# Attention and expert layer on one core: operand addresses, accumulator banks, and where work at the two seams of the kernel stands

## The chip, the core and the metric

The kernel runs on one core of one Trainium2 chip. The core has a matrix engine (TensorE, "PE" in the profile, with its weight loads as "PEld"), a vector engine (VectorE, "DVE"), a scalar engine (ScalarE, "ACT"), GpSimd ("POOL") and a sync engine that issues most of the transfers ("SP"). The metric is the device time of one execution in microseconds (us), lower is better. Matrix products write to PSUM, eight banks of 512 fp32 numbers in each of 128 partitions; all other tiles lie in SBUF.

## The reference

```python
def _attn_ref(u, v, z):                       # 8 x 2496 x 256, z: 8 x 2496 x 64
    scores = (1.0 / S) * np.matmul(z, z.transpose(0, 2, 1))
    attn = np.maximum(scores, 0.0) ** 2
    return u * np.matmul(attn, v)

def _moe_ref(x, modality_id, w_gate, modality_bias, w1, w2):   # 19968 tokens, 8 experts
    logits = x @ w_gate + modality_bias[modality_id]
    e_idx = np.argmax(logits, axis=1)
    probs = softmax(logits)                   # with 1e-9 added to the sum
    gate_w = probs[np.arange(N), e_idx]
    for e in range(E):
        mask = e_idx == e
        h = np.maximum(x[mask] @ w1[e], 0.0)  # 256 x 1024
        out[mask] = gate_w[mask, None] * (h @ w2[e])
```

The attention's output, as 19968 rows of 256, is the input of the expert layer. Each token goes to one expert.

## The kernel before

**Precision.** Every fp32 operand of a product is split into a high part (rounded to fp32r) and a low part (the rest), and a product is the sum of three: high x high, high x low, low x high. So everything that feeds TensorE needs a cast (high, on ACT or DVE) and a subtraction (low, on DVE).

**Phase 1, attention.** A batch's 2496 rows are five chunks of 512 queries (the last one 448). A step `g` is one batch, one chunk, and two blocks of 128 keys; there are ten steps to a chunk, 400 in all. A step has these pieces:

- `scores(g)`: six matmuls (three pairs, one of each pair on either half of the rows) into one PSUM tile `s` of two banks, then a relu on ACT into `r` (L275).
- `square(g)` on ACT (L281), `high(g)` (`ah`, ACT or DVE, L288), `low(g)` (`al`, DVE, L297).
- `weigh(g)`: 24 products (L313) of `ah`, `al` with the value parts `vh`, `vl`, into four accumulators of one bank each: two halves of the model dimension (`dh`) times two halves of the rows (`r`). The first step of a chunk goes through all terms of `dh` = 0 first and then those of `dh` = 1; the others are sorted by operand.

At a chunk's end `evacuate_low` copies the two accumulators with `r` = 1 to SBUF (ACT, L355), `evacuate_high` adds the two with `r` = 0 (DVE, L359), `make_rows` turns the result by 16 matmuls (L389) into two PSUM tiles `po`, and `take_rows` multiplies by `u` (DVE, L399). Then `logits` computes the gate's logits on DVE, two products with an accumulated sum to a call (L411), 16 calls to a chunk. When a batch's logits are there, routing finds every token's slot among its expert's rows, and indirect transfers on POOL scatter the rows to a buffer `xs` in HBM (L524).

**PSUM.** `ps_s` holds `s` (two banks), `ps_a` six banks under one tag. `bank_tile` draws from `ps_a` for the accumulators, the `po` tiles, the small products of routing (`pc`), and the target of the products of zeros at the start (`warm`, L863). A tile waits for the last reader of the bank that it gets.

**Order.** The order on PE, ACT, DVE and POOL is the program's order (a manual schedule). Steps look ahead: later steps' scores are issued before a step's products, and at steps 1, 14 and 16 (`DEEPER`) the distance grows by one, so that one more `scores` is issued inside `weigh`, ahead of its last terms. Pieces beside the steps (evacuation, logits, splits of the next batch, routing) stand in a list `waiting` with a step by which they are due; `beside` places them by an estimated clock for ACT and DVE. What is left when the steps end is issued at once.

**Phase 2, experts.** 39 tiles of up to 512 tokens go through `run_tile`. The first four (t = -4 to -1) belong to the expert with most tokens so far, and start before the last tokens are routed. Slot `f` of a tile issues `up` (six matmuls, L983, relu into `hh` on ACT, L987, rest into `hl` on DVE, L988) for one eighth of the hidden width, then `down` of slot f - 2 (matmuls L996 and L997). `up` takes its PSUM tile from four banks. There are three sets of weight tiles; set 0 serves the tiles before t = 0 and every third after it. Weights are split in four parts each (`part_weights_high` on ACT, `part_weights_low` on DVE, L813): parts 0 and 1 are w1, 2 and 3 are w2. The first set is split in the last steps of phase 1. The list `between` holds work that is issued beside the first four tiles, by slot: the last chunk's rows (`make_last_rows`, L371, `take_last_rows`), its logits, two calls to a slot from slot 2 on, the routing of the last batch, and the planning of the remaining tiles.

**SBUF.** Pools stand one behind the other: `const`, `small`, `turned` (the `zm` tiles), `rows`, then `bulk` with `r`, `vh`, `vl`, `ah`, `al`. In phase 2 `mp` (`hh`, `hl` and others) and behind it `wp` (weight sets 1 and 2) take the place of `bulk`. Weight set 0 lies at the other end. A tile takes a multiple of 32 bytes of a partition.

The lines at the start of phase 1 that the change touches:

```python
        warm = [bank_tile([P, T], "warm") for _ in halves]
        for n in range(11):
            for x, h in zip(warm, halves):
                nc.tensor.matmul(out=x, lhsT=zeros[h, 0:P], rhs=zeros[h, :], start=True, stop=True)
```

Of the kernel before, what the change touches and what calls it, by code (L numbers as in the profile page):

```python
# [9 lines left out]
F32 = mybir.dt.float32  # L10
# [3 lines left out]
ALU = mybir.AluOpType  # L14
# [12 lines left out]
def tile_attention_moe(ctx: ExitStack, tc: tile.TileContext, u, v, zt, mid, wg, mb, w1, w2, out):  # L27
# [53 lines left out]
    turned = ctx.enter_context(tc.tile_pool(name="turned", bufs=1))  # L81
    rows = ctx.enter_context(tc.tile_pool(name="rows", bufs=1))
    bulk = ph1.enter_context(tc.tile_pool(name="bulk", bufs=1))
    raw = feed.enter_context(tc.tile_pool(name="raw", bufs=1, side="right"))
    ps_s = ph1.enter_context(tc.tile_pool(name="ps_s", bufs=1, space=PSUM))
    ps_a = ph1.enter_context(tc.tile_pool(name="ps_a", bufs=6, space=PSUM))
    bank = {"pool": ps_a, "tag": "acc"}

    def bank_tile(shape, name):
        return bank["pool"].tile(shape, F32, tag=bank["tag"], name=name)  # L90
# [172 lines left out]

    def scores(g):
        b, c, i = steps[g]
        w = width[c]
        s = ps_s.tile([P, 2, T], F32, tag="s", name="s")
        mv = Z[b, c]
        for n, (kl, ql) in enumerate(((0, 1), (1, 0), (0, 0)) if g else ((0, 0), (0, 1), (1, 0))):
            for t in range(2):  # L270
                k = 2 * i + t
                lhs = Z[b, k // J][halves[t], kl, (k % J) * P:(k % J + 1) * P]
                nc.tensor.matmul(out=s[:, t, :w], lhsT=lhs, rhs=mv[halves[t], ql, :w], start=n == 0, stop=n == 2)  # L273
        r = bulk.tile([P, 2, T], F32, tag="a", bufs=3, name="r")
        nc.scalar.activation(out=r[:, :, :w], in_=s[:, :, :w], func=AF.Relu, scale=INV)  # L275
        st_s[g] = r

    def square(g):
        w = width[steps[g][1]]
        a = st_s.pop(g)  # L280
        nc.scalar.square(out=a[:, :, :w], in_=a[:, :, :w])  # L281
        st_a[g] = a

    def high(g):
# [20 lines left out]
    def weigh(g, inside=()):  # L305
# [3 lines left out]
        if i == 0:  # L309
            acc[b, c] = list(zip(*([bank_tile([P, T], "acc") for _ in range(2)] for _ in range(KD))))  # L310

# [11 lines left out]
        terms = [(dh, x, y) for dh in range(KD) for x, y in ((ah, 0), (ah, 1), (al, 0))]  # L323
        if i:
            terms.sort(key=lambda t: (t[1] is al, t[2]))
        for m, (dh, x, y) in enumerate(terms):
            if m == len(terms) - KD:
                for n in inside:
                    scores(n)
            for k in (2 * i, 2 * i + 1)[:1 if last else 2]:  # L330
                for r in range(2):
                    product(r, dh, k, x, y)
        if last:
# [213 lines left out]
    def choose():  # L547

        cnt = t8("c_cnt")
        nc.vector.tensor_tensor(out=cnt, in0=base[one], in1=base0[one], op=ALU.subtract)  # L550
        most = small.tile([1, 1], F32, name="c_most")
        nc.vector.tensor_reduce(out=most, in_=cnt, axis=AX.X, op=ALU.max)
        val = t8("c_val")
        nc.vector.scalar_tensor_tensor(out=val, in0=cnt, scalar=most, in1=em8[one], op0=ALU.is_equal, op1=ALU.mult)
        who = small.tile([1, 1], F32, name="c_who")
        nc.vector.tensor_reduce(out=who, in_=val, axis=AX.X, op=ALU.min)
        nc.vector.tensor_scalar(
            out=skip, in0=em8[one], scalar1=who, scalar2=float(EARLY * T), op0=ALU.is_equal, op1=ALU.mult
        )
        at = small.tile([1, 2], F32, name="c_at")  # L560
        nc.vector.tensor_scalar(out=at[:, 0:1], in0=who, scalar1=float(E), scalar2=None, op0=ALU.add)
        nc.vector.tensor_scalar(out=at[:, 1:2], in0=at[:, 0:1], scalar1=float(CAP), scalar2=None, op0=ALU.mult)
        nc.vector.tensor_copy(out=first, in_=at)
# [287 lines left out]
    for q in range(KD + 2):  # L851
        queue(G - 8 + q, G - 4 + q, act(1.05, part_weights_high, -1, q), dve(1.25, part_weights_low, -1, q))
    queue(G - 6, G - 4, dve(1.2, turn_blocks, -EARLY), act(1.05, part_high, -EARLY), dve(1.25, part_low, -EARLY))
# [5 lines left out]
    with tc.manual_schedule(engines={ET.PE, ET.Activation, ET.DVE, ET.Pool}):  # L859
        warm = [bank_tile([P, T], "warm") for _ in halves]  # L860
        for n in range(11):
            for x, h in zip(warm, halves):
                nc.tensor.matmul(out=x, lhsT=zeros[h, 0:P], rhs=zeros[h, :], start=True, stop=True)  # L863
# [4 lines left out]
        prep_v_low(0, 0)  # L868
        square(0)
        by[0] = "D"  # L870
        high(0)
        low(0)
        scores(1)
        load_z(0, 3)
# [81 lines left out]
        for h in reversed(range(KD)):  # L956
            evacuate_high(B - 1, NCH - 1, h)
        waiting += [(end, g, p) for g in sorted(due) for end, p in due[g]]
        while waiting:
            waiting = [(0, 0, p) for _, _, p in waiting]  # L960
            beside(G, True)
# [140 lines left out]
    def put(slot, *pieces):  # L1102
        n, f = slots[slot]
        between[n][f] += pieces

    for n in range(LGN):
        put(2 + n // 2, lambda n=n: logits(B - 1, NCH - 1, n))
# [74 lines left out]
```

## Time and profile before

| | |
|---|---|
| median of three runs | 2264.76 us (2263.47 to 2266.08) |
| the profiled execution | 2264.21 us |
| its span in the trace | 2262.4 us |
| phase 1, to the last product | 0 to 1352 us |
| phase 2 | 1352 to 2262 us |
| PE, DVE, ACT, POOL busy | 99%, 80%, 70%, 16% of the span |
| granted clock of TensorE | 0.996 |

How to read the lines of the views. A line of the timeline is: start in us, length in us, engine, line of the kernel, operation, output <- inputs, number of instructions merged, and in brackets the idle time of the engine just before and what ended it. Matmuls overlap, so the distance between two starts says more than a length. A line of the waits is: engine, line, what was waited for, then total us, times, longest us. A line of the windows is: the stretch, its length, busy us and number of instructions of PE, PEld, DVE, ACT and POOL, then the granted clock of TensorE (1.00 is full), the share of the transfer engines, and GB/s. In the view of one source line, the last part lists who waited for that line's instructions: us in total and times.

### The profile page before, as it was taken

How to read it: one execution, taken by the hardware profiler on the slowest of the kernel's cores; microseconds unless marked ns; L12 is line 12 of the kernel's file. 1: busy time of each engine (PE TensorE's matmuls, PEld its weight loads, DVE VectorE, ACT ScalarE, POOL GpSimd, SP SyncE). 2: the span in 40 equal slices, each digit the busy share in tenths (PEclk: the TensorE clock that was granted, in tenths of full speed). 3: DMA queues.
4: the chain of work that ended last, by engine and by line, in shares of the span. 5: the costliest groups of instructions: out<-in, count | busy, mean ns of one | idle time of the engine just before them, and what ended most of it. 6: DMA issues, size and time to landing. Idle time of an engine off the chain costs nothing.

```text
span 2262.4 us, 44477 instructions
## 1 busy us (share of the span) xinstructions
PE 2237.1 (99%) x16880; PEld 2025.0 (90%) x16880; DVE 1805.4 (80%) x4550; ACT 1573.2 (70%) x1911; POOL 368.7 (16%) x349
## 2 busy tenths in 40 slices
PE   9999999999999999999999999999999999999996
PEld 7788999999999999999999888888888888888885
DVE  7889989989989989989989998666666666666663
ACT  7888888888888888888888873454545455555452
POOL 0000210220210210220220422211111111111111
PEclk9999999999999999999999999999999999999998
DMA  5222223222012112112111122654545454544440
GB/s 186 107 66 92 93 88 108 80 72 79 32 59 74 34 56 75 37 55 72 39 47 37 55 86 59 185 157 123 157 124 157 127 153 129 151 132 149 135 139 23
DMA packets 199603, 216.64 MB, mean 96 GB/s; under 512 B 118449, under 2 KB 166065, under 8 KB 194513
## 3 DMA queue, kind: packets, MB, share of 16 engines
q1 hardware_dynamic: 184288, 172.49, 26.4%
q0 software_dynamic: 15088, 41.21, 4.9%
q8 instruction: 134, 2.20, 0.4%
q14 instruction: 93, 0.75, 0.1%
HBM read 168.23 MB, written 62.19 MB: 102 GB/s over the span
## 4 chain that ended last, share of the span: by engine, by line
PE 58%; issue 26%; DMA 9%; POOL 3%; DVE 2%; ACT 1%; POOLq 0%; SPq 0%; DVEq 0%; ACTq 0%
PE acc L313 42%; PE s L273 11%; DMA out_dram<-y,ids 9%; POOL out_dram L1015 3%; PE ph L983 1%; PE po L996 1%; PE po L389 1%; DVE spare L411 1%; PE po L997 1%; DVE al L297 0%; POOL xs L524 0%; ACT r L275 0%; DMA xs<-x,sloti 0%; DVE x L359 0%; PE warm L863 0%
## 5 line engine op out<-in xcount | busy, mean ns | idle before, releaser
L275 ACT ACTIVATE r<-s 128x1024 f32<-128x1024 f32 (+1 forms) x400 | 403.0, 1008 | 196.4 <-PE s L273 194.2
L297 DVE TENSOR_TENSOR al<-r,ah 128x1024 fp32r<-128x1024 f32 (+1 forms) x360 | 431.2, 1198 | 87.1 <-ACT ah L288 69.7
L313 PE MATMUL acc<-ah,vh 64*128 64x512 f32 (+1 forms) x3120 | 498.0, 385 | 0.8 <-DVE ah L288 0.8
L313 PE MATMUL acc<-ah,vl 64*128 64x512 f32 (+1 forms) x3120 | 490.2, 383 | 0.0
L313 PE MATMUL acc<-al,vh 64*128 64x512 f32 (+1 forms) x3120 | 488.5, 383 | 0.1
L411 DVE SCALAR_TENSOR_TENSOR spare<-x,wgb 128x256 f32<-128x256 f32 x1280 | 462.3, 420 | 1.0
L987 ACT ACTIVATE hh<-ph 128x512 fp32r<-128x512 f32 x312 | 186.7, 598 | 396.5 <-PE ph L983 396.4
L996 PE MATMUL po<-w,hh 128*128 128x512 f32 x1256 | 456.1, 397 | 0.0
L983 PE MATMUL ph<-xh,w 128*128 128x512 f32 x1248 | 431.2, 396 | 3.1 <-DVE hl L988 3.1
L281 ACT ACTIVATE r<-r 128x1024 f32<-128x1024 f32 (+1 forms) x400 | 416.6, 1042 | 3.5
L313 PEld LDWEIGHTS acc<-ah,vh 64*128 64x128 f32 x3120 | 386.3, 185 | 19.2 <-ACT x L355 1.7
L313 PEld LDWEIGHTS acc<-al,vh 64*128 64x128 f32 x3120 | 383.5, 185 | 17.0 <-DVE al L297 0.5
L313 PEld LDWEIGHTS acc<-ah,vl 64*128 64x128 f32 x3120 | 382.4, 185 | 16.8
L988 DVE SCALAR_TENSOR_TENSOR hl<-ph,hh 128x512 fp32r<-128x512 f32 x312 | 215.4, 691 | 227.1 <-ACT hh L987 227.1
L273 PE MATMUL s<-zm 64*128 64x512 f32 (+1 forms) x2400 | 391.5, 387 | 2.3 <-ACT r L275 2.3
L524 POOL DMA_INDIRECT xs<-x,sloti x160 | 208.9, 1306 | 1020.3 <-DVE x L522 976.0
L997 PE MATMUL po<-w,hl 128*128 128x256 f32 x1256 | 356.3, 284 | 0.0
L273 PEld LDWEIGHTS s<-zm 64*128 64x128 f32 x2400 | 294.2, 185 | 16.1 <-ACT r L275 4.2
L996 PEld LDWEIGHTS po<-w,hh 128*128 128x128 f32 x1256 | 237.0, 189 | 58.0
L288 ACT CAST ah<-r 128x1024 fp32r<-128x1024 f32 (+1 forms) x283 | 288.2, 1018 | 0.0
L983 PEld LDWEIGHTS ph<-xh,w 128*128 128x128 f32 x1248 | 234.6, 188 | 59.2 <-DVE hl L988 3.3
L1015 POOL DMA_INDIRECT out_dram<-y,ids x157 | 152.8, 973 | 702.5 <-DVE y L1013 678.0
(151 smaller groups left out, 1974.0 us busy)
## 6 DMA issues: line engine op xcount, KB each, us to landing
w<-w1s SPq DMA_DIRECT2D x37, 1024.0 KB
w<-w2s SPq DMA_DIRECT2D x37, 1024.0 KB
xg<-xs SPq DMA_DIRECT2D x156, 128.0 KB
vr<-in_v_dram SPq DMA_DIRECT2D x32, 512.0 KB
ut<-in_u_dram SPq DMA_DIRECT2D x32, 512.0 KB
zr<-in_zt_dram SPq DMA_DIRECT2D x40, 256.0 KB
w1s<-in_moe_w_dram SPq DMA_DIRECT2D x16, 512.0 KB
w2s<-in_moe_w_dram SPq DMA_DIRECT2D x8, 1024.0 KB
```

The costliest lines, as they stand in the source:

```text
L273: nc.tensor.matmul(out=s[:, t, :w], lhsT=lhs, rhs=mv[halves[t], ql, :w], start=n == 0, stop=n == 2)
L275: nc.scalar.activation(out=r[:, :, :w], in_=s[:, :, :w], func=AF.Relu, scale=INV)
L281: nc.scalar.square(out=a[:, :, :w], in_=a[:, :, :w])
L288: copy(out=ah[:, :, :w], in_=st_a[g][:, :, :w])
L297: nc.vector.tensor_tensor(out=al[:, :, :w], in0=a[:, :, :w], in1=ah[:, :, :w].bitcast(F32), op=ALU.subtract)
L313: nc.tensor.matmul(out=acc[b, c][r][dh][:, :w], lhsT=V[b, k // J][y][halves[r], k % J, dh * P:(dh + 1) * P], rhs=x[halves[r], k % 2, :w], ...
L411: nc.vector.scalar_tensor_tensor(out=spare[:, k % 2, :], in0=x[:, j, 0:D], scalar=1.0, in1=wgb[:, e, :], op0=ALU.mult, op1=ALU.mult, accum ...
L983: nc.tensor.matmul(out=ph, lhsT=lhs, rhs=rhs[:, k, :], start=n == 0, stop=n == 3 * KD - 1)
L988: nc.vector.scalar_tensor_tensor(out=hl, in0=ph, scalar=0.0, in1=hh.bitcast(F32), op0=ALU.max, op1=ALU.subtract)
L996: nc.tensor.matmul(out=po[j], lhsT=hh[:, s], rhs=both, start=f == 0, stop=False, skip_group_check=True)
L997: nc.tensor.matmul(out=po[j][:, 0:D], lhsT=hl[:, s], rhs=w[:, 0, :], start=False, stop=f == KF - 1, skip_group_check=True)
L1015: nc.gpsimd.indirect_dma_start(out=out, out_offset=bass.IndirectOffsetOnAxis(ap=ids[:, j:j + 1], axis=0), in_=y, in_offset=None, bounds_ch ...
```

## The change

- `ps_a` has four banks instead of six and serves the accumulators alone. A new pool `ps_t` of two banks serves what `bank_tile` gives out in phase 1.
- `scores(g, more=True)` takes two single banks from `ps_t` instead of the tile `s`, and does the relu in two pieces. It is used for step 1 and for the scores inside `weigh`.
- Step 0 goes in halves: relu and square of each half in turn on ACT, then `first_parts` casts and subtracts each half on DVE, and `weigh(0)` does all terms of the first key block before those of the second.
- Eight pairs of products of zeros at the start instead of eleven.
- The low parts 2 and 3 of the first weight set are no longer split in phase 1 but in slots 0 and 3 of the first expert tile. Calls of `logits` that are left when the steps end go to slots 4, 5, 5, 7, 7, 7 of that tile.
- A tile `room` of 32 bytes is added at the head of `rows`, and three small tiles of `choose` become parts of one, which takes 64 bytes from `small`. Together the tiles of `bulk` and `mp` begin 32 bytes earlier.

```diff
+    rows.tile([P, 8], F32, name="room")
...
-    ps_a = ph1.enter_context(tc.tile_pool(name="ps_a", bufs=6, space=PSUM))
-    bank = {"pool": ps_a, "tag": "acc"}
+    ps_a = ph1.enter_context(tc.tile_pool(name="ps_a", bufs=4, space=PSUM))
+    ps_t = ph1.enter_context(tc.tile_pool(name="ps_t", bufs=2, space=PSUM))
+    bank = {"pool": ps_t, "tag": "po"}
...
-    def scores(g):
+    def scores(g, more=False):
...
-        s = ps_s.tile([P, 2, T], F32, tag="s", name="s")
+        if more:
+            s = [bank_tile([P, T], "s") for _ in halves]
+        else:
+            both = ps_s.tile([P, 2, T], F32, tag="s", name="s")
+            s = [both[:, t, :] for t in range(2)]
...
-        nc.scalar.activation(out=r[:, :, :w], in_=s[:, :, :w], func=AF.Relu, scale=INV)
+        if more or not g:
+            for t in range(2):
+                nc.scalar.activation(out=r[:, t, :w], in_=s[t][:, :w], func=AF.Relu, scale=INV)
+                if not g:
+                    nc.scalar.square(out=r[:, t, :], in_=r[:, t, :])
+        else:
+            nc.scalar.activation(out=r[:, :, :w], in_=both[:, :, :w], func=AF.Relu, scale=INV)
...
+    def first_parts():
+
+        a = st_s.pop(0)
+        ah, al = (bulk.tile([P, 2, T], F32R, tag=n, bufs=AHEAD, name=n) for n in ("ah", "al"))
+        for t in range(2):
+            nc.vector.tensor_copy(out=ah[:, t, :], in_=a[:, t, :])
+            nc.vector.tensor_tensor(out=al[:, t, :], in0=a[:, t, :], in1=ah[:, t, :].bitcast(F32), op=ALU.subtract)
+        st_h[0] = (ah, al)
...
-            acc[b, c] = list(zip(*([bank_tile([P, T], "acc") for _ in range(2)] for _ in range(KD))))
+            acc[b, c] = list(zip(*([ps_a.tile([P, T], F32, tag="acc", name="acc") for _ in range(2)] for _ in range(KD))))
...
-        if i:
+        if i or not g:
             terms.sort(key=lambda t: (t[1] is al, t[2]))
...
+        tiles = (2 * i, 2 * i + 1)[:1 if last else 2]
+        for ks in (tiles,) if g else ((k,) for k in tiles):
+            for m, (dh, x, y) in enumerate(terms):
+                if m == len(terms) - KD and 2 * i in ks:
+                    for n in inside:
+                        scores(n, True)
+                for k in ks:
+                    for r in range(2):
+                        product(r, dh, k, x, y)
...
-        most = small.tile([1, 1], F32, name="c_most")
+        one_of = small.tile([1, 4], F32, name="c_most")
+        most, who, at = one_of[:, 0:1], one_of[:, 1:2], one_of[:, 2:4]
...
-        queue(G - 8 + q, G - 4 + q, act(1.05, part_weights_high, -1, q), dve(1.25, part_weights_low, -1, q))
+        lower = (dve(1.25, part_weights_low, -1, q),) if q < KD else ()
+        queue(G - 8 + q, G - 4 + q, act(1.05, part_weights_high, -1, q), *lower)
...
-        for n in range(11):
+        for n in range(8):
...
-        square(0)
-        by[0] = "D"
-        high(0)
-        low(0)
-        scores(1)
+        first_parts()
+        scores(1, True)
...
+        left_over = [q[2][0][3] for q in waiting if q[2][0][2] is logits]
+        waiting = [q for q in waiting if q[2][0][2] is not logits]
...
+    put(0, lambda: part_weights_low(-1, KD))
+    put(3, lambda: part_weights_low(-1, KD + 1))
+    for n, args in enumerate(left_over):
+        put((4, 5, 5, 7, 7, 7)[min(n, 5)], lambda args=args: logits(*args))
```

## What is predicted, and why

> **What bounds the kernel now.** The page comes first, then the waits of PE, then one window over the attention loop.
>
> ```profile
> PE 2237.1 (99%) x16880; PEld 2025.0 (90%) x16880; DVE 1805.4 (80%) x4550; ACT 1573.2 (70%) x1911; POOL 368.7 (16%) x349
> ...
> PE ph L983 <- DVE hl L988: 3.1, 1, 3.1
> PE s L273 <- ACT r L275: 2.3, 4, 1.1
> ...
> 13.00:1352.00 1339.00, 1337.62 (x12382) 1271.31 (x12378) 1204.63 (x3631) 1131.60 (x1247) 198.08 (x164) 1.00 0.22 70
> ```
>
> TensorE (PE) is busy in 99% of the span. From 13 to 1352 us it is idle for 1.4 us in all, at full clock, though DVE is 90% busy there. So PE bounds the loop, and any wait put ahead of one of its matmuls lengthens the time by its full length, since nothing later can be caught up. What can be won from waits is small: 3.1 us where the expert tiles begin, 2.3 us ahead of scores, and the lead-in before 13 us.
>
> The working below is against the profiled execution: 2264.21 us, of which the trace shows 2262.4. That is 0.55 us under the median of the three runs, 2264.76, so the same forecast holds against either.
>
> **The start.**
>
> ```profile
> 1.47 4.70 PE L863 MATMUL warm<-zeros 64*128 64x512 f32 x22 [1.47 <-DVE zeros L95]
> ...
> 6.00 0.86 PE L273 MATMUL s<-zm 64*128 64x512 f32 x6
> 6.90 1.02 ACT L275 ACTIVATE r<-s 128x1024 f32<-128x1024 f32 x1 [2.68 <-PE s L273]
> ...
> 9.80 0.73 PE L313 MATMUL acc<-ah,vh 64*128 64x512 f32 x4 [0.85 <-DVE ah L288]
> ...
> 11.02 0.60 ACT L228 CAST zm<-zr 128x512 fp32r<-128x512 f32 x1
> 11.65 0.69 DVE L233 TENSOR_TENSOR zm<-zr,zm 128x512 fp32r<-128x512 f32 x1 [0.65 <-ACT zm L228]
> ...
> 13.02 0.86 PE L273 MATMUL s<-zm 64*128 64x512 f32 x6
> ```
>
> Eleven pairs of zero products take 4.70 us, 0.43 a pair at most; three fewer let scores(0) start near 5.1 instead of 6.0, and its relu near 6.2 instead of 6.9. Four half-size pieces on ACT (0.6 us each, the row of the 512-wide cast) reach the first half of `ah` near 7.8, so the first product starts about 1.9 us earlier and weigh(0) ends near 10.6 instead of 13.0. But scores(2) needs the second chunk of z, and ACT reaches that cast behind the relus and squares of steps 0 and 1: six 512-wide pieces and one 1024-wide where four 1024-wide ones stood, 6 x 0.6 + 1.0 against 4.1, some 0.5 us more work begun 0.7 us earlier. With DVE's part it lands near 12.15 instead of 11.65 + 0.69 = 12.34. So scores(2) starts 13.02 - 12.15 = 0.9 us earlier, and the rest of the 1.9 is lost again. **-0.9 us**, bounds 0 and -2.5.
>
> **The accumulators' banks.** This is the term that decides. Six banks were shared by accumulators (four to a chunk) and by everything else. The pool gives out first what was released first. So a new chunk's dh = 0 pair got the two banks that nobody held, and only its dh = 1 pair, six pairs of products later, needed the two that `evacuate_low` (ACT, L355) had emptied. Now the pool has four banks, all held by the chunk before. By the same order of release dh = 0 gets the two banks that `evacuate_low` frees, and dh = 1 the two that `evacuate_high` (DVE, L359) frees. How late these come is seen at a boundary inside a batch, at one between batches, and at the first and the last of the 39:
>
> ```profile
> 214.36 0.62 PE L313 MATMUL acc<-ah,vl 64*128 64x512 f32 x2
> ...
> 214.98 1.05 ACT L355 COPY x<-acc 128x512 f32<-128x512 f32 x2
> 215.28 0.85 PE L313 MATMUL acc<-ah,vh 64*128 64x512 f32 x4
> ...
> 216.06 1.29 DVE L359 TENSOR_TENSOR x<-acc,x 128x512 f32<-128x512 f32 x2 [1.77 <-ACT x L355]
> ...
> 181.08 0.63 PE L313 MATMUL acc<-ah,vh 64*128 64x512 f32 x4
> ...
> 181.57 0.95 ACT L355 COPY x<-acc 128x448 f32<-128x448 f32 x2
> ...
> 44.60 1.06 ACT L355 COPY x<-acc 128x512 f32<-128x512 f32 x2
> ...
> 45.12 0.62 PE L313 MATMUL acc<-ah,vh 64*128 64x512 f32 x4
> ...
> 1323.70 1.05 ACT L355 COPY x<-acc 128x512 f32<-128x512 f32 x2
> ...
> 1324.37 0.57 PE L313 MATMUL acc<-ah,vh 64*128 64x448 f32 x4
> ...
>   PEld acc L313: 1.7, 7
> ```
>
> Inside a batch the copies start as the old chunk's last product ends and are over at 216.03; the new chunk's first product starts at 215.28, after one group of scores. It would have to wait 0.75 us. At the first boundary it is 45.66 - 45.12 = 0.54, at the last 1324.75 - 1324.37 = 0.38; I take 0.68 for the 32 of this kind. Between batches ACT comes to the copies later: 182.52 - 181.08 = 1.44. The last row, from the view of line 355, says who waited for these copies: weight loads of L313, 7 times, 1.7 us. Those are the dh = 1 products, 1.37 us behind the first (six pairs at the 0.2275 us worked out under Addresses), so at seven boundaries the copies end about 1.37 + 1.7/7 = 1.6 us after the first product. I take 1.5 for seven. Sum: 32 x 0.68 + 7 x 1.5 = 32.3 us. To each of the 39 comes about 0.15 us, an estimate: 0.04 for the semaphore's way, and 0.11 for a restart, by which the four products after a wait (9.80, 0.73 us) outlast four in a stream (45.12, 0.62 us). That is 6 us: **+38 us**. The second wait, dh = 1 on `evacuate_high`, is just met: 217.35 in the row, against 216.09 + 1.37 = 217.46. Behind the waiting product stand all other products and the next scores, and behind these relu, square and the parts on ACT and DVE; these move along and gain nothing. Bounds: if every boundary costs what the shortest does (0.38 + 0.06), 17 us; if every one costs the longest (1.6 + 0.2), 70 us. The rows sit near 0.7, so for the range I keep 26 to 44.
>
> **Scores inside a step.** At steps 1, 14 and 16 an extra scores(n) runs inside the products, and the next step's scores waited until ACT had read it; steps 14 and 16 look alike:
>
> ```profile
> 62.42 1.01 ACT L275 ACTIVATE r<-s 128x1024 f32<-128x1024 f32 x1
> ...
> 63.49 0.96 PE L273 MATMUL s<-zm 64*128 64x512 f32 x6 [0.48 <-ACT r L275]
> ```
>
> With banks of its own the extra one holds up nobody. The list has four such waits, 2.3 us; 1.1 is the start's, and the 1.2 left are twice 0.48 and step 1: **-1.2 us**. No make_rows holds those two banks at those steps. ACT does the relu in two pieces, 0.2 us more; if that comes late, the gain is half.
>
> **The first expert tile.**
>
> ```profile
> 1351.57 2.35 DVE L813 TENSOR_TENSOR w<-w 128x1024 fp32r<-128x1024 f32 x2
> 1353.85 1.15 DVE L359 TENSOR_TENSOR x<-acc,x 128x448 f32<-128x448 f32 x2
> ...
> 1354.98 0.42 DVE L411 SCALAR_TENSOR_TENSOR spare<-x,wgb 128x256 f32<-128x256 f32 x1
> ...
> 1358.50 1.28 DVE L988 SCALAR_TENSOR_TENSOR hl<-ph,hh 128x512 fp32r<-128x512 f32 x2
> ...
> 1359.23 0.51 PE L983 MATMUL ph<-xh,w 128*128 128x512 f32 x1 [3.09 <-DVE hl L988]
> ...
> 1360.00:1364.00 4.00, 4.00 (x14) 3.30 (x13) 2.35 (x6) 0.60 (x1) 0.00 (x0) 0.59 0.81 148
> ```
>
> DVE splits two weight parts (2.35 us), evacuates, then does ten logit products, that is five calls (3.5 us), before the first `hl`. PE waits 3.1 us, and its granted clock then falls to 0.59 over four microseconds, another 4 x 0.41 = 1.6. Moved into the tile, the same 5.9 us of DVE work stands behind `hl` of slots 0 to 7, so the wait and the slow clock go: -4.7. What is late next is DVE in slots 5 to 7: `hl` 0.6, two calls of the last chunk's logits 1.4, up to two moved calls 1.4, and the next tile's transpose and split 1.2 each, against 2.8 us of PE a slot. Slot by slot this leaves `hl` of slot 7 about 1.3 us late, and the next tile's split as much; nothing of it if the planner places some calls earlier in the time freed. Between -4.7 + 2.6 and -4.7 I take **-3.5 us**, bounds -1.5 and -5.
>
> **Addresses.** By the sizes in the code, the attention operands (vh, vl, ah, al) and hh, hl began 32 bytes past a multiple of 64; zm began at a multiple. The 64 bytes saved in `small` and the 32 of `room` move the former to multiples. The weights w1, w2 of two of the three sets, stacked behind them, move off theirs by the same 32 bytes; the third set was off and stays. The trace holds both kinds:
>
> ```profile
> 55.29 0.85 PE L273 MATMUL s<-zm 64*128 64x512 f32 x6
> ...
> 55.97 1.08 PE L313 MATMUL acc<-ah,vh 64*128 64x512 f32 x8
> ...
> 57.80 1.08 PE L313 MATMUL acc<-al,vh 64*128 64x512 f32 x8
> ...
> 58.71 0.85 PE L273 MATMUL s<-zm 64*128 64x512 f32 x6
> ...
> 1898.70 0.40 PE L983 MATMUL ph<-xh,w 128*128 128x512 f32 x1
> ...
> 1921.15 0.39 PE L983 MATMUL ph<-xh,w 128*128 128x512 f32 x1
> ...
> 1943.72 0.39 PE L983 MATMUL ph<-xh,w 128*128 128x512 f32 x1
> ```
>
> Scores, at multiples: (55.97 - 55.29) / 3 = 0.227 us a pair. Products, off them: (58.71 - 57.80) / 4 = 0.2275. No difference. Of two expert tiles, the one whose weights lie off the multiple takes 22.45 us, the one with weights on it 22.57: if anything the wrong way round. I take **0**. Bounds: 0.5% of 2200 us, which is the tiles' difference, either way: 11 us.
>
> The Trainium skill, page "SBUF — State Buffer", section "Specifications (TRN2)", gives the line as 16 bytes, and both kinds of address begin such a line. By that rule the edit is worth nothing, and the rival below that rests on it gets less; the rows above agree (0.227 and 0.2275 us).
>
> **At nothing.** The two moved weight parts are of w2, which `down` first reads in slot 2; `up` of slots 0 to 2, 4.2 us, hides them, and without that cover they cost their 2.35 us. The shared row of `choose` has the same instructions. `route_count` gets the two banks that were the free ones before. No DMA and nothing on SP or POOL is moved.
>
> **Sum.** 38 - 0.9 - 1.2 - 3.5 + 0 = +32.4. 2264.2 + 32.4, about **2296 us**, 1.4% slower.
>
> **Rivals.** *No wait at the boundaries* (faster): the new products find their banks emptied in time, because a chunk's copies begin before its last products end. The stopping products of the two low banks come first in the last step, so ACT could start up to 0.6 us sooner; the rows speak against it, the copies start at 214.98 just as the last product ends, behind a square. Then only the gains are left: 2264.2 - 5.6 = 2258.6. It decides if the copies end 0.7 us sooner than now. *Address pace* (faster): products on multiples run a pair faster. Break-even is 32 us over the 5,880 pairs of the loop, 5.5 ns of 227. At 2% in both phases, four times what the two tiles differ, it gives 2296 - 44 = 2252. Against it are the equal paces above. *Waits and clock* (slower still): if the idle time at boundaries also lowered the clock as after 1359, 39 x 1.6 = 62 us more, 2358. The lead-in holds the longest wait on r, 1.1 us, and kept its clock:
>
> ```profile
> 6.00:10.00 4.00, 2.04 (x16) 1.08 (x14) 1.74 (x3) 3.06 (x3) 0.00 (x0) 1.00 1.01 390
> ```
>
> *The change does not do what it says at the tile*: the late DVE work costs as much as before, +3.5: 2300, in the range.
>
> **Chances.** Forecast 0.76; no wait 0.10; pace 0.11; clock 0.03. About 0.2% (4.5 us) is what a measurement of this kernel can tell from no change. Faster by more takes most of the two fast rivals: 0.18. Within it 0.06, slower 0.76. The forecast's own range is 2275 to 2310, from the boundary term's 26 to 44 and the addresses' 11 either way, not both at their ends. To reach 8 in 10 the range goes down to the no-wait rival: 2257 to 2310.
>
> **What will show it.** Right: PE's waits list L313 acc behind ACT L355, some 39 times, 0.4 to 1.7 us each, 30 us or more together; the view of line 355 names PE as the one that waits. Scores behind r vanish from the list but for the start; the wait on hl shrinks under 2 us and no window after 1352 shows a clock of 0.6. Four pairs of products stay at 0.91 us. Wrong: PE busy without a break at the boundaries, or groups of eight products well under 0.90 us.

## The result, and the profile after

| | before | after |
|---|---|---|
| median, runs on the same chip | 2264.11 us (2263.09 to 2266.08) | 2277.87 us (2277.01 to 2278.44) |
| span of the profiled execution | 2262.4 us | 2276.0 us |

The changed kernel takes 1.0059 times as long, with a 95% interval of 1.0042 to 1.0077. It is slower, as forecast, but by 13.8 us, where 32 were forecast. The two spans differ by 13.6 us. Cut at the same instructions in both traces (each stretch from the start of one product to the start of another), they divide so:

| stretch | before | after | difference | forecast |
|---|---|---|---|---|
| start to the last product of chunk 0 | 44.20 | 42.82 | -1.38 | start, -0.9 |
| 39 boundaries: last product of a chunk to the first `dh` = 1 product of the next | 82.03 | 112.47 | +30.44 | banks, +38 |
| the rest of the chunks | 1225.56 | 1220.07 | -5.49 | scores in a step, -1.2; addresses, 0 |
| first expert tile | 28.34 | 24.02 | -4.32 | -3.5 |
| other 38 tiles to the end, and the 0.29 us ahead of the first | 882.00 + 0.29 | 876.36 + 0.29 | -5.64 | addresses, 0 |

The last row's 882.00 is 22.70 for the second tile, 811.07 for the 36 behind it, and 48.23 for the last and the end; after, 22.57 + 805.38 + 48.41.

First the page of after: the busy times, then two groups of line 335, the products (L313 before).

```profile
PE 2247.5 (99%) x16874; PEld 2029.5 (89%) x16874; DVE 1807.1 (79%) x4552; ACT 1574.1 (69%) x1917; POOL 360.6 (16%) x349
...
L335 PE MATMUL acc<-ah,vh 64*128 64x512 f32 (+1 forms) x3120 | 530.1, 387 | 8.4 <-ACT x L379 7.1
...
L335 PEld LDWEIGHTS acc<-ah,vh 64*128 64x128 f32 x3120 | 399.7, 184 | 48.0 <-ACT x L379 32.3
```

PE is still "99% busy", and its idle time behind the copies is 7.1 us only. The loss stands in the weight loads: they wait 32.3 us for L379, the copies of `evacuate_low`. A matmul whose weights are late can count as busy while it waits. Next, who waited for those copies, from the view of line 379, and the waits of PE:

```profile
  DVE x L383: 34.8, 31
  PEld acc L335: 32.3, 78
  PE acc L335: 7.1, 8
```

```profile
PE acc L335 <- ACT x L379: 7.1, 8, 0.9
...
PE acc L335 <- DVE ah L302: 1.1, 1, 1.1
PE s L280 <- ACT r L288: 0.3, 1, 0.3
...
PE po L1020 <- DVE hl L1011: 0.2, 1, 0.2
```

Before, weight loads waited 7 times, 1.7 us. Now it is 78 times, twice at each of the 39 boundaries. The wait of 3.1 us on `hl` has become 0.2, and the four on `r` have become one of 0.3. One boundary in the timeline of after, the one that the prediction quotes of before:

```profile
214.99 1.03 PE L280 MATMUL s<-zm 64*128 64x512 f32 x6
215.36 1.05 ACT L379 COPY x<-acc 128x512 f32<-128x512 f32 x2
215.98 0.18 PEld L335 LDWEIGHTS acc<-ah,vh 64*128 64x128 f32 x1 [0.39 <-ACT x L379]
215.98 1.22 PE L335 MATMUL acc<-ah,vh 64*128 64x512 f32 x4
...
216.46 0.29 PEld L335 LDWEIGHTS acc<-ah,vh 64*128 64x128 f32 x3 [0.30 <-ACT x L379]
...
217.73 0.84 PE L335 MATMUL acc<-ah,vh 64*128 64x512 f32 x4
```

And the rows of before that it is to be compared with:

```profile
214.59 1.07 PE L273 MATMUL s<-zm 64*128 64x512 f32 x6
215.28 0.85 PE L313 MATMUL acc<-ah,vh 64*128 64x512 f32 x4
...
216.65 0.84 PE L313 MATMUL acc<-ah,vh 64*128 64x512 f32 x4
```

Before, the first product came 0.69 us after the scores (215.28 - 214.59) and the first one of `dh` = 1 another 1.37 us on (216.65). Now it is 0.99 and 1.75 us: 0.30 for the first copy, 0.38 for the second, 0.68 together.

### The profile page after: what moved, and what is told of

It reads as the page before. It is cut to its first block, busy times and chain, and to the rows that moved or that the text cites. A ratio compares the mean times of both kernels' runs of the same rounds, so it can differ in the third digit from the quotient of the medians.

```text
span 2276.0 us, 44472 instructions
## 1 busy us (share of the span) xinstructions
PE 2247.5 (99%) x16874; PEld 2029.5 (89%) x16874; DVE 1807.1 (79%) x4552; ACT 1574.1 (69%) x1917; POOL 360.6 (16%) x349
## 4 chain that ended last, share of the span: by engine, by line
PE 61%; issue 25%; DMA 9%; POOL 3%; ACT 1%; DVE 1%; POOLq 0%; ACTq 0%; DVEq 0%
PE acc L335 46%; PE s L280 12%; DMA out_dram<-y,ids 9%; POOL out_dram L1038 3%; PE ph L1006 1%; PE po L413 1%; PE po L1019 1%; ACT r L288 0%; ACT r L294 0%; DVE spare L435 0%; PE po L1020 0%; POOLq L1038 0%; PE warm L887 0%; ACT x L379 0%; ACT r L284 0%
## 5 line engine op out<-in xcount | busy, mean ns | idle before, releaser
L335 PE MATMUL acc<-ah,vh 64*128 64x512 f32 (+1 forms) x3120 | 530.1, 387 | 8.4 <-ACT x L379 7.1
L335 PE MATMUL acc<-ah,vl 64*128 64x512 f32 (+1 forms) x3120 | 511.8, 382 | 0.0
L335 PE MATMUL acc<-al,vh 64*128 64x512 f32 (+1 forms) x3120 | 506.7, 382 | 0.0
L1019 PE MATMUL po<-w,hh 128*128 128x512 f32 x1256 | 450.0, 394 | 0.0
L335 PEld LDWEIGHTS acc<-ah,vh 64*128 64x128 f32 x3120 | 399.7, 184 | 48.0 <-ACT x L379 32.3
L335 PEld LDWEIGHTS acc<-ah,vl 64*128 64x128 f32 x3120 | 403.6, 184 | 14.0
L335 PEld LDWEIGHTS acc<-al,vh 64*128 64x128 f32 x3120 | 403.0, 184 | 14.2
L280 PE MATMUL s<-zm 64*128 64x512 f32 (+1 forms) x2400 | 405.7, 385 | 0.8 <-ACT r L288 0.3
L548 POOL DMA_INDIRECT xs<-x,sloti x160 | 200.8, 1255 | 1052.5 <-DVE x L546 1006.9
L280 PEld LDWEIGHTS s<-zm 64*128 64x128 f32 x2400 | 310.8, 185 | 8.5 <-ACT r L288 0.8
```

What stands on the lines that cost most here:

```text
L280: nc.tensor.matmul(out=s[t][:, :w], lhsT=lhs, rhs=mv[halves[t], ql, :w], start=n == 0, stop=n == 2)
L335: nc.tensor.matmul(out=acc[b, c][r][dh][:, :w], lhsT=V[b, k // J][y][halves[r], k % J, dh * P:(dh + 1) * P], rhs=x[halves[r], k % 2, :w], ...
L1019: nc.tensor.matmul(out=po[j], lhsT=hh[:, s], rhs=both, start=f == 0, stop=False, skip_group_check=True)
```

## The experiments

Each was timed beside the kernel before on the same chip; from chip to chip that kernel took 2263.7 to 2264.7 us. "Six banks" means the pool of before, shared by accumulators and the rest.

**1. The change with six banks.**

```diff
-    ps_a = ph1.enter_context(tc.tile_pool(name="ps_a", bufs=4, space=PSUM))
-    ps_t = ph1.enter_context(tc.tile_pool(name="ps_t", bufs=2, space=PSUM))
-    bank = {"pool": ps_t, "tag": "po"}
+    ps_a = ph1.enter_context(tc.tile_pool(name="ps_a", bufs=6, space=PSUM))
+    bank = {"pool": ps_a, "tag": "acc"}
```

> The changed kernel with the one pool of six shared banks again; all else of the change kept. If the boundary waits are what made it slower (the theory: 30.4 us of them in the two traces), PE's waits on L379 vanish, the way from a chunk's last product to its successor's seventh pair falls from 2.7 us back to about 2.1, and the time is 2278 - 30 = 2248 us, 0.7% faster than the kernel before. If the split only took part of it (rival: six banks would also have slowed the longer look-ahead's scores), it stays above 2255.

Measured: 2245.32 us (2244.86 to 2245.57), ratio 0.9913, 0.9897 to 0.993. The boundaries are back at 81.38 us. The busy times and the same weight loads on its page:

```profile
PE 2221.0 (99%) x16874; PEld 2017.6 (90%) x16874; DVE 1804.5 (80%) x4552; ACT 1573.5 (70%) x1917; POOL 366.7 (16%) x349
...
L334 PEld LDWEIGHTS acc<-ah,vh 64*128 64x128 f32 x3120 | 384.6, 184 | 18.5 <-ACT x L378 1.7
```

The weight loads wait 1.7 us again, and 26.5 us of "busy" PE (2247.5 - 2221.0) are gone with the same number of instructions: that was waiting. Without the split of the banks, the change is 19 us faster than before; the split costs 2277.87 - 2245.32 = 32.5.

**2. The split of the banks alone, on the kernel before.**

```diff
-    ps_a = ph1.enter_context(tc.tile_pool(name="ps_a", bufs=6, space=PSUM))
-    bank = {"pool": ps_a, "tag": "acc"}
+    ps_a = ph1.enter_context(tc.tile_pool(name="ps_a", bufs=4, space=PSUM))
+    ps_t = ph1.enter_context(tc.tile_pool(name="ps_t", bufs=2, space=PSUM))
+    bank = {"pool": ps_t, "tag": "po"}
...
-            acc[b, c] = list(zip(*([bank_tile([P, T], "acc") for _ in range(2)] for _ in range(KD))))
+            acc[b, c] = list(zip(*([ps_a.tile([P, T], F32, tag="acc", name="acc") for _ in range(2)] for _ in range(KD))))
```

> The kernel before with only the banks split, four for the accumulators and two for the rest. Theory: +30 us, 2294 to 2296, waits of PE on the copies at 39 boundaries. My own sum in the prediction said +38 (2302). Rival, that the waits come from the change's other edits: within 5 us of 2264.

Measured: 2297.65 us (2297.11 to 2298.1), ratio 1.0144, 1.0127 to 1.0161; boundaries 112.16 us. From both sides the split costs 32 to 33 us, of which 30 to 31 stand at the boundaries; 2.4 us (experiment 1 against the change) to 2.9 (here against before) stand in the rest of the chunks.

**3. The second copy of a chunk on DVE, on the changed kernel.**

```diff
-        nc.scalar.copy(out=oT[b, c][0][:, h, :w], in_=acc[b, c][1][h][:, :w])
+        copy = nc.vector.tensor_copy if h else nc.scalar.copy
+        copy(out=oT[b, c][0][:, h, :w], in_=acc[b, c][1][h][:, :w])
```

> The changed kernel (2277.9 us), with four banks for the accumulators as there, but the second of the two low copies of a chunk made by DVE instead of ACT, so that both run side by side. Theory: the products of a new chunk wait for the copies alone; DVE is idle when they start, so the second bank is free some 0.4 to 0.5 us sooner, and the first product of the second half no longer waits: boundaries 112 us become 95, the kernel 2259 to 2264. Rival: the wait is set by the DVE additions behind the copies, or by the pool, and then the boundaries stay near 112 or grow by the 0.6 us that DVE comes later to the additions: 2278 to 2300.

Measured: 2283.59 us (2281.57 to 2284.26), ratio 1.0083, 1.0069 to 1.0096; boundaries 117.09 us. The theory missed. Two lines of its waits of PE, and the boundary shown above in its timeline:

```profile
PE acc L335 <- ACT x L380: 7.1, 8, 0.9
PE acc L335 <- DVE x L380: 6.8, 8, 0.9
```

```profile
215.93 0.87 PE L335 MATMUL acc<-ah,vh 64*128 64x512 f32 x4
...
217.41 0.78 PE L335 MATMUL acc<-ah,vh 64*128 64x512 f32 x4
```

Where DVE was idle, as here, the second wait did go: `dh` = 1 starts 1.48 us behind the first product instead of 1.75. At eight boundaries DVE came late and PE waited up to 0.9 us for it. The wait is for the copies, whoever makes them, but DVE isn't free when they are due.

**4. The addresses alone, on the kernel before.**

```diff
+    rows.tile([P, 8], F32, name="room")
...
-        most = small.tile([1, 1], F32, name="c_most")
+        one_of = small.tile([1, 4], F32, name="c_most")
+        most, who, at = one_of[:, 0:1], one_of[:, 1:2], one_of[:, 2:4]
...
```

> The kernel before with only the 32 bytes of room and the shared row of choose, so that vh, vl, ah, al, hh, hl begin at multiples of 64 and weight sets 1 and 2 begin 32 past one. Theory after the two traces: a step of the loop goes from 3.43 to 3.40 us and an expert tile from 22.55 to 22.38, 10 to 13 us less in all, 2252 to 2254. The prediction's value was 0 (2264). Rival, that the pace rose because the waits at boundaries gave other engines time: no change here.

Measured: 2251.83 us (2251.42 to 2253.12), ratio 0.9945, 0.9928 to 0.9961. This is the term that I valued at nothing: -12.8 us. In the two traces 6.25 us of it stand in the rest of the chunks and 5.6 in the 38 expert tiles behind the first. Scores in two successive steps of its timeline:

```profile
54.69 0.85 PE L274 MATMUL s<-zm 64*128 64x512 f32 x6
...
58.09 0.85 PE L274 MATMUL s<-zm 64*128 64x512 f32 x6
```

A step of fifteen pairs takes 3.40 us, 0.2267 a pair; before it was 58.71 - 55.29 = 3.42. An expert tile takes 22.33 to 22.40 us; before it was 22.45 to 22.60.

**5. The change without `room`.**

```diff
-    rows.tile([P, 8], F32, name="room")
```

> The changed kernel without room: vh, vl, ah, al, hh, hl 32 past a multiple of 64 again, weight sets 1 and 2 on multiples, zm where the change has it. If the residue of these operands sets the pace, 10 to 13 us more than the change, about 2290, with steps of 3.43 us. If it was the 64 bytes by which zm moved, as the change: 2278.

Measured: 2290.95 us (2290.74 to 2291.34), ratio 1.0116, 1.0099 to 1.0132, 13.1 us over the change.

```profile
54.87 1.02 PE L279 MATMUL s<-zm 64*128 64x512 f32 x6
...
58.29 1.02 PE L279 MATMUL s<-zm 64*128 64x512 f32 x6
```

3.42 us again. So 32 bytes decide, and the shared row of `choose` by itself brings nothing.

**6 and 7. Which operand?** The kernel of experiment 4, with 32 bytes more ahead of `ah`, `al`; then with 32 bytes ahead of `vh` and another 32 ahead of `ah`.

```diff
         prep_v_low(0, 0)
+        bulk.tile([P, 8], F32, name="shift")
         square(0)
```

> The kernel before with its addresses moved as in the change (2251.8 us so far), and 32 bytes more between vl and ah: vh and vl, the stationary operands of the products, stay on multiples of 64, ah and al, the moving ones, go 32 bytes off. The expert phase is unchanged. Theory 'stationary': only where the weight load begins counts, so the chunks keep their 1219 us and the kernel takes 2252. Theory 'moving': only where the moving rows begin counts, so the chunks go back to 1225.5 and the kernel to 2258. Theory 'both': between them, 2255.

```diff
+        bulk.tile([P, 8], F32, name="shift")
         prep_v_high(0, 0, nc.vector.tensor_copy)
         prep_v_low(0, 0)
+        bulk.tile([P, 8], F32, name="back")
         square(0)
```

> The mirror image: vh and vl 32 bytes off, ah and al on multiples of 64, the expert phase unchanged. Theory 'stationary': the chunks go back to 1225.5 us and the kernel to 2258. Theory 'moving': it stays at 2252. Theory 'both': 2255.

Measured: 2275.78 us (2274.68 to 2276.54), ratio 1.0049, 1.0035 to 1.0062, and 2278.55 us (2278.39 to 2280.65), ratio 1.0065, 1.0051 to 1.0078. None of the theories held: with one operand off, either one, it is slower than before, where both were off. Steps of the first, then of the second:

```profile
55.90 0.85 PE L274 MATMUL s<-zm 64*128 64x512 f32 x6
...
59.40 0.86 PE L274 MATMUL s<-zm 64*128 64x512 f32 x6
```

```profile
54.24 0.86 PE L274 MATMUL s<-zm 64*128 64x512 f32 x6
...
57.74 0.86 PE L274 MATMUL s<-zm 64*128 64x512 f32 x6
```

3.50 us. That gave a new theory: what counts is not where an operand begins but whether the operands begin alike.

**8. The expert weights on multiples of 64 as well, on the kernel of experiment 1.**

```diff
         weight_tiles(pool, 0)
+        pool.tile([P, 8], F32, name="shift")
...
     head.append(wp)
+    wp.tile([P, 8], F32, name="shift2")
```

> The changed kernel with six shared banks (2245.3 us so far), and the three sets of expert weights moved by 32 bytes, so that all of them begin on multiples of 64 (in the change all three lie off). In the expert tiles w1 is the stationary operand of 48 matmuls of a tile and w2 the moving one of 64. Theory 'stationary': hl and hh, stationary in 64 matmuls, gave about 0.15 us a tile when they moved, so w1 gives up to 48/64 of that, 0.11 us, over 36 tiles 4 us: 2241. Theory 'moving': w2 gives about as much as hh and hl did, 5 us: 2240. If neither the expert weights count: 2245.3 and tiles of 22.33 to 22.41 us as before; if the mean of the two sides counts more than multiples of 64 (128-byte places), the tiles go back up, 2248.

Measured: 2239.34 us (2238.53 to 2240.94), ratio 0.9892, 0.9876 to 0.9907. That is the lowest median of the study, but the runs of experiments 9, 12 and 14 overlap with these. The starts of three expert tiles, first in after, then here:

```profile
1847.22 0.39 PE L1006 MATMUL ph<-xh,w 128*128 128x512 f32 x1
...
1869.55 0.40 PE L1006 MATMUL ph<-xh,w 128*128 128x512 f32 x1
...
1891.95 0.40 PE L1006 MATMUL ph<-xh,w 128*128 128x512 f32 x1
```

```profile
1812.53 0.39 PE L1007 MATMUL ph<-xh,w 128*128 128x512 f32 x1
...
1834.77 0.39 PE L1007 MATMUL ph<-xh,w 128*128 128x512 f32 x1
...
1857.01 0.39 PE L1007 MATMUL ph<-xh,w 128*128 128x512 f32 x1
```

22.33 and 22.40 us a tile become 22.24 for every set. The two theories stood at 2240 and 2241 us, so the run doesn't choose between them.

**9. Everything off.** The kernel of experiment 8, all operands 32 bytes on (the right side's weights stay where they were in after).

```diff
     turned = ctx.enter_context(tc.tile_pool(name="turned", bufs=1))
+    turned.tile([P, 8], F32, name="odd")
...
-        pool.tile([P, 8], F32, name="shift")
```

> The kernel of the last experiment with all expert weights on multiples of 64 (2239.3 us), and every operand of every matmul moved 32 bytes on: scores, products, experts alike lie 32 bytes off a multiple of 64, and none on one. Theory 'alike': the pairs lose time only where operands on a multiple and operands off it follow or face each other, as the two mixed experiments showed, so all off is as fast as all on: 2239, chunks 1218 us, expert tiles 22.24. Theory 'multiples': an operand has to begin on a multiple of 64, and then the loop gives back at least the 6 us and the tiles the 10 us that the moves have won: 2256 or more.

Measured: 2240.55 us (2240.21 to 2240.89), ratio 0.9894, 0.9879 to 0.991.

```profile
54.40 0.84 PE L280 MATMUL s<-zm 64*128 64x512 f32 x6
...
57.80 0.84 PE L280 MATMUL s<-zm 64*128 64x512 f32 x6
```

3.40 us with no operand on a multiple of 64, and expert tiles of 22.24: "alike" held, "multiples" fell.

**10 to 12. Alike by how much?** The kernel of experiment 8, with a gap ahead of `ah` and `al`: 64 bytes, 128 bytes and 256 bytes. With the first two the expert weights move by as much; with the third they stay.

The cut shown is that of experiment 10; the sizes 24, 16 and 24 are 40, 32 and 40 in experiment 11, and 8, 64 and 8 in experiment 12.

```diff
-        pool.tile([P, 8], F32, name="shift")
+        pool.tile([P, 24], F32, name="shift")
...
         prep_v_low(0, 0)
+        bulk.tile([P, 16], F32, name="gap")
         first_parts()
...
-    wp.tile([P, 8], F32, name="shift2")
+    wp.tile([P, 24], F32, name="shift2")
```

> The kernel with all operands on multiples of 64 (2239.3 us) has them all 64 bytes past a multiple of 128. Here ah and al go 64 bytes on, against zm, vh and vl, and so do the expert weights, against xh, hh and hl; every operand still begins on a multiple of 64. Theory 'alike by 64': no change, 2239 us, steps of 3.40, expert tiles of 22.24. Theory 'alike by 128': the moved operands are unlike the rest as in the two mixed experiments, so the chunks grow by up to 24 us and the tiles by some 0.1 to 0.3 each, 2245 to 2275. Attention and experts are judged apart, from their own stretches.

> The kernel with all operands on multiples of 64 (2239.3 us). There every operand begins 64 bytes past a multiple of 128; by 256 the attention operands and xh, hh, hl all leave 64, the expert weights 192. Here ah and al go 128 bytes on and so do the expert weights: by 128 all is still alike; by 256 the attention is now mixed (64 and 192), and the experts are alike (all 64). Theory 'alike by 128': nothing changes, chunks 1217 us, expert tiles 22.24, 2239. Theory 'alike by 256': the chunks grow by 10 to 25 us, as with the other mixtures, and the expert tiles come under 22.24, towards the pace of the attention (226.7 ns instead of 231 for a product of 512 columns: 22.0 or less). Attention and experts are judged apart.

> The same kernel with ah and al alone 256 bytes on: alike by 256, not by 512 (64 and 320). Theories 'alike by 128' and 'alike by 256': no change, 2239 us, steps of 3.40. Theory 'the same place in a longer stretch, or the plain distance, counts': the chunks grow by 10 us or more.

Measured: 2262.72 us (2260.67 to 2263.04; ratio 0.9991, 0.9982 to 1.0), 2262.66 us (2261.52 to 2263.58; 0.9995, 0.9986 to 1.0004), and 2240.15 us (2239.86 to 2240.48; 0.9897, 0.9882 to 0.9912). Steps with 64, 128 and 256 bytes:

```profile
54.56 0.87 PE L279 MATMUL s<-zm 64*128 64x512 f32 x6
...
58.02 0.87 PE L279 MATMUL s<-zm 64*128 64x512 f32 x6
```

```profile
55.15 0.88 PE L279 MATMUL s<-zm 64*128 64x512 f32 x6
...
58.64 0.88 PE L279 MATMUL s<-zm 64*128 64x512 f32 x6
```

```profile
53.58 0.85 PE L279 MATMUL s<-zm 64*128 64x512 f32 x6
...
56.98 0.85 PE L279 MATMUL s<-zm 64*128 64x512 f32 x6
```

3.46, 3.49 and 3.40 us. In the attention, operands lose nothing when they begin at the same place within 256 bytes. All variants, by that place (the first byte in a partition, modulo 256) and by the third row of the first table; the change and what is built on it, 5 and 8 to 12, have some 1.7 us less there for other reasons, the scores inside a step, and the change and 5 have some 2.4 us more, from the split of the banks (1220.07 in the change, 1217.63 in experiment 1):

| kernel | `zm` | `vh`, `vl` | `ah`, `al` | rest of the chunks, us |
|---|---|---|---|---|
| before | 128 | 96 | 96 | 1225.56 |
| 4 | 64 | 64 | 64 | 1219.31 |
| 6 | 64 | 64 | 96 | 1242.72 |
| 7 | 64 | 96 | 128 | 1244.84 |
| the change | 64 | 64 | 64 | 1220.07 |
| 5 | 64 | 32 | 32 | 1226.36 |
| 8 | 64 | 64 | 64 | 1217.62 |
| 9 | 96 | 96 | 96 | 1216.88 |
| 10 | 64 | 64 | 128 | 1232.93 |
| 11 | 64 | 64 | 192 | 1238.04 |
| 12 | 64 | 64 | 64 | 1216.96 |

In the expert tiles (those behind the first four) the rule by 256 fails: in experiment 11 all operands began at 64, and a tile took 22.25 us as against 22.24 with weights at 192; in experiment 10, with weights at 0 and at 128, it took 22.30 and 22.46. Alike by 128 is enough there in the cases tried, and a mixture costs 0.05 us (22.29 in experiment 10) to 0.36 (22.60 in experiment 5). What orders the mixtures stays open.

**13. The late logits and the two weight parts put back, on the kernel of experiment 1.**

```diff
-        lower = (dve(1.25, part_weights_low, -1, q),) if q < KD else ()
-        queue(G - 8 + q, G - 4 + q, act(1.05, part_weights_high, -1, q), *lower)
+        queue(G - 8 + q, G - 4 + q, act(1.05, part_weights_high, -1, q), dve(1.25, part_weights_low, -1, q))
...
-        left_over = [q[2][0][3] for q in waiting if q[2][0][2] is logits]
-        waiting = [q for q in waiting if q[2][0][2] is not logits]
...
-    put(0, lambda: part_weights_low(-1, KD))
-    put(3, lambda: part_weights_low(-1, KD + 1))
-    for n, args in enumerate(left_over):
-        put((4, 5, 5, 7, 7, 7)[min(n, 5)], lambda args=args: logits(*args))
```

> The changed kernel with six shared banks (2245.3 us), and the two weight parts and the late logits put back ahead of the first expert tile. My theory: DVE does 5.9 us of them before the first hl, PE waits about 3 us and its clock falls, so the first tile is 4.3 us longer, 2249 to 2250, and a window after the last chunk shows a granted clock near 0.6. Rival: the planner places those calls elsewhere now, and the first tile gains under 1.5 us by the move: 2246 to 2247.

Measured: 2247.28 us (2245.48 to 2247.46), ratio 0.9921, 0.9908 to 0.9935; the first tile is 27.07 us instead of the 25.45 of experiment 1. Its waits, and its windows from the start of the tile:

```profile
PE ph L1002 <- DVE hl L1007: 1.6, 1, 1.6
PE ph L1002 <- DVE x L382: 1.5, 1, 1.5
```

```profile
1342.00:1346.00 4.00, 2.48 (x14) 1.52 (x11) 4.00 (x10) 1.56 (x3) 2.04 (x3) 1.00 0.09 33
1346.00:1350.00 4.00, 2.35 (x15) 1.84 (x14) 4.00 (x20) 0.60 (x1) 0.83 (x1) 1.00 0.13 39
1350.00:1354.00 4.00, 4.00 (x20) 3.32 (x20) 2.20 (x5) 0.60 (x1) 0.00 (x0) 1.00 0.78 148
```

Half a miss: the wait on `hl` is back with 1.6 us, but the clock stays at 1.00. The other wait, for a bank that the last chunk's addition frees, is in experiment 1 as well (1.4 us), so it isn't the price of the move.

**14. Eleven pairs of zeros, on the kernel of experiment 8.**

```diff
-        for n in range(8):
+        for n in range(11):
```

> The same kernel (2239.3 us) with eleven pairs of zero products again instead of eight. Theory: PE is what the first scores wait for, so they start some 0.6 us later and the whole time is 0.4 to 0.7 us longer, 2239.9. Rival: chunk 1 of z, through ACT, sets the third step anyway, and nothing changes, under 0.2 us: 2239.3. A second rival: with fewer zeros PE was slower at first, and the time is the same or shorter by up to 0.5.

Measured: 2241.84 us (2239.97 to 2241.95), ratio 0.9897, 0.9882 to 0.9912. That interval overlaps with the one of experiment 8, so the medians decide nothing between 0 and 2 us. In the traces, one execution of each, the last product of chunk 0 starts at 44.71 us here, and at 42.57 to 43.46 in experiments 1, 8, 9, 12 and 13 with eight pairs.

## Why the prediction was right in its sign and wrong in its size

**What bounds it: right.** No time lost on PE in the loop was made up later: experiments 1 and 2 give the 30 us at the boundaries back, or add them, in full in the total, with 1 to 3 us more. The measured 2277.87 us still lies in the forecast's own range, 2275 to 2310, but only because that range left room at both of the terms that missed.

**The start: right.** Forecast -0.9, measured -1.38 to the end of chunk 0's products, with the first wait on `r` (1.1 us before) gone. The first rows after the scores:

```profile
7.77 0.73 PE L335 MATMUL acc<-ah,vh 64*128 64x512 f32 x4 [1.12 <-DVE ah L302]
...
11.76 0.73 PE L280 MATMUL s<-zm 64*128 64x512 f32 x4 [0.23 <-DVE zm L235]
```

The first product came 9.80 - 7.77 = 2.0 us earlier (1.9 forecast), and `scores(2)` had to wait for chunk 1 of z until 11.76 us (12.15 forecast), which took part of it back. How much of it the zeros are isn't settled: by the traces of experiment 14 up to some 2 us, by its medians 0 to 2. Executions that start alike differ by 0.9 us here (42.57 to 43.46), so the term is right only within that; 0.5 of it is in the trace of experiment 4 as well, which moves nothing but addresses.

**The banks: mechanism right, size too large.** Both copies are waited for at all 39 boundaries. The step "to each of the 39 comes about 0.15 us, for the semaphore's way and a restart" is the one that failed. Without it the sum was 32.3 us; the trace has 30.4, as 19.7 at 32 boundaries inside a batch, 0.61 each (0.68 forecast), and 10.8 at the seven between batches, 1.54 each (1.5 forecast). At 215.98 the first product starts within 0.1 us of the end of the first of the two copies, which began at 215.36 and share 1.05 us; there is no dearer restart in it. `evacuate_high`, "just met" in the forecast, cost little. Who waited for it, from the view of line 383:

```profile
  PEld acc L335: 3.5, 16
```

At 16 boundaries weight loads waited for it, 0.2 us each. The split as a whole costs 33.0 us (experiment 2), since 2.4 to 2.9 us stand behind the boundaries, where the forecast had nothing; whether they are these waits wasn't tried.

**Scores inside a step: right.** The waits on `r` are 0.3 us instead of 2.3, and chunk 1, with steps 14 and 16, is 1.78 us shorter behind its boundary in experiment 1 and 0.10 in experiment 4: about -1.7 by the edits to the scores, -1.2 forecast with step 1.

**The first tile: right in its sum, less so in its parts.** Forecast -3.5, measured -4.32. The clock is full all through the tile, which lasts from 1375.65 to 1399.67 us in after, as the window over it says:

```profile
1375.60:1399.70 24.10, 23.87 (x122) 19.71 (x121) 23.28 (x85) 7.50 (x13) 2.15 (x3) 1.00 0.37 72
```

But putting the pieces back cost 1.6 us of tile in experiment 13, not 4.3. There the wait came in two pieces of 1.6 and 1.5 us with matmuls between, and the clock did not fall; before, one of 3.1 was followed by 0.59. So the move is worth 1.6; experiment 13 without it is 28.34 - 27.07 = 1.3 under the kernel before, with the clock at full speed; and the change is 25.45 - 24.02 = 1.4 under experiment 1, whose wait for a bank of the last chunk its list doesn't have. Why the wait came in pieces wasn't tried by itself.

**The addresses: wrong, and the largest miss.** "No difference. I take 0" is the step that failed. Experiments 4 and 5 give -12.8 and -13.1 us, just past the bound of 11. The reasoning compared scores with products inside one step, and one expert tile with another, and took equal pace for no effect. But every step of the kernel before mixed operands at 128 and at 96, so its trace held no step without the loss: 3.42 us where 3.40 is possible. The two expert tiles that it compared were mixtures too (22.45 and 22.57 us where 22.24 is possible), and 5.6 of the 12.8 us come from such tiles, by an order that stays open. Two kinds of operand in one mixed stream can't show what the mixture costs. The Trainium skill's rule in "SBUF — State Buffer", section "Specifications (TRN2)", by which the move was worth nothing, leaves this out; the measurement decides. The rival *Address pace* had the right sign with the wrong reason: in the attention not multiples of 64 but operands that begin alike, and 0.6% over the whole kernel instead of its 2%.

The terms add up: +33.0 for the split, -12.8 for the addresses, and -6.5 for the start, the scores and the first tile (experiment 1 against 4) make +13.7, and 13.8 were measured. Of the 18.7 us between the forecast's +32.4 and these, 12.8 are the addresses, 38 - 33.0 = 5.0 the banks, and 0.9 the rest.

## What to carry to other kernels

Where PE is full, give the accumulators of the next group banks that nobody holds; the copies that free the others then hide under its first products, and a weight load's wait in the profile is the place to look when they don't. A price of zero read from a trace in which every case is mixed is no measurement: build the unmixed case, or keep the bound wide. The best kernel here is the change with one pool of six banks and the expert weights moved as in experiment 8, 2239.34 us, 1.1% faster than before; experiments 9 and 12 are within 1.3 us of it.

## What the runs showed of the hardware that was not expected

- A pair of fp32r products on the two halves of the rows, 512 columns each, takes 226.7 ns where all operands of the attention begin at the same place modulo 256 bytes (3.40 us for fifteen). Where the moving operand begins 32 to 128 bytes elsewhere than the stationary one, the mean pair of the steps shown takes 231 to 233 (3.46 to 3.50 us). Where the two operands of every matmul lie alike, but those of the scores elsewhere than those of the products (before, 128 and 96), it takes 228 (3.42 us). Pairs of scores, whose own operands lie alike, slow down too: by their starts in the trace of experiment 6, the three of the step at 55.90 us take 230, 235 and 229 ns. Whether the place is on a multiple of 64 made no difference.
- In products over all 128 rows the operands' places matter less clearly: 22.24 us a tile (behind the first four) where all begin alike by 128 bytes, 22.25 where alike by 256, and 22.29 to 22.60 otherwise.
- The granted clock fell to 0.59 after one wait of 3.1 us, and stayed at 1.00 through waits of 1.5 and 1.6 us four microseconds apart.
